# Agent attention with a grouped mixture of experts: another order for the first sorted tile, the placements, the maximum's chain and the factor loads

## The chip, the cores and the metric

The kernel runs on one core of one Trainium2 chip. Its five engines (PE for matmuls, DVE, ACT, POOL, and SP, which here only starts DMAs) run their own instruction streams side by side and wait for each other through semaphores. The metric is the device time of one execution in microseconds (us); lower is better. Every line number of the form L1582 is one of the kernel before, unless a listing of the changed kernel is meant.

## The reference

Four batches of 10048 tokens with 128 channels and 49 agents go through an attention in two steps. Its result, all 40192 rows, goes through a grouped mixture of experts with 4 groups of 4 experts, of which each row uses one:

```python
a2k = sm(agents, k)              # softmax over the 10048 keys, per agent
agent_v = a2k @ v                # 49 x 128
q2a = sm(q, agents)              # softmax over the 49 agents, per token
x = q2a @ agent_v
...
# g: argmax of x @ w_group; e: argmax of x @ w_expert[g]
out = g_w * e_w * (relu(x @ w1[g, e]) @ w2[g, e])
```

## The kernel before

The batches are taken in the order `SEQ = (1, 2, 3, 0)`. The first three are "own" batches. In such a batch all 20 tiles of 512 tokens go through the batch's most common expert, tile by tile, and the rows of other experts are dealt with at the very end. Since x is a mix of 49 agent values, the agent values are folded into w1: the kernel multiplies rows of exponentials (49 high and 49 low halves, so 98) by a folded w1, and what has been left out of the softmax and the gates is one factor per token, applied at the end. The last batch (`SORTED`) is routed instead: its rows are written in the order of their experts into `sorted_rows` in DRAM, and read back as 22 sorted tiles.

**A unit** is 128 of the 1024 hidden columns of one tile. Its first step is two matmuls into a PSUM bank `ph<-et,wbuf`; ACT makes the relu `hh`, DVE the low half `hl` (its "eviction", after which the bank is free; there are three such banks), and the second step is three matmuls `po<-hh` x2 and `po<-hl`. The second step of a unit comes eight units after its first (`LAG`). Tiles 11 to 19 of the third own batch, and the sorted tiles, run their units in groups of four. Three own batches make 480 units.

**Beside the units** everything else is made: scores and maxima of the next batch's keys (`key_scores`, `key_max`), the subtraction of the maximum from them (`value_less`, DVE `S<-S,mb`), exponentials, products with v, the query rows (`query_split`, L939) and their turning (`turned`, L1001), the choice of experts, and the placements. Each is a generator, a lane, and a planner at build time (`advance`, L1902) steps them after each unit. `clock[0]` counts units. A step that yields a number waits for that many units; `lag()` is 2. A lane may step when it is behind its share (`QUEUE`, `TOTALS`), within a budget of time per unit on DVE and ACT. The Tile framework then puts the instructions into each engine's stream.

**The maximum's chain** (`key_max`, L485) ends the score pass of a batch: DVE reduces to `mx`, PE transposes it (`at<-cp,mx`), DVE reduces again and makes `dg`, PE spreads it to all partitions, and only then can the subtractions and with them the value steps begin.

**Placements** (`placing`, L1378, DMA at L1384): each of the 79 blocks of 128 rows is written by one indirect DMA that POOL issues. They are the lane p3, which `advance` steps apart from the others, in four of five units and at the end in five of eight:

```python
if y["live"] and part > y["start"] and (clock[0] % 5 if part < NOWN - 1 + GROUPED / OT else clock[0] % 8 not in (0, 3, 6)):
    step(y)
```

**The end of the own batches** is prepared by `ahead` (L2037): when the last agent lane has ended, it queues the weights of the first sorted tiles (`weights`, `next_weights`, L1571: `wbuf<-wdr`, in halves, one half every `APART` = 4 units). When no lane is live, it issues four fetches of sorted tiles at once (`begin`, `fetch`, L1582: `er<-sorted_rows`, 512 tokens each). From the sixth unit after that, it turns one tile at a time (`next_turn`, `turn`: four transposes on PE `at<-ident,er`, a copy on ACT, strips by DMA at L1596), until two are turned. A fetch reads any row of its tile, so it comes after all placements. The first sorted unit comes some 30 units later.

**Output of an own tile:** `factors` (L1684) loads the per-token factors, spread to all partitions, into a buffer `oo` (L1698, `oo<-cwt`); after the last unit of the tile `out_rows` (L1701) multiplies `po` into it on DVE (`oo<-po,oo`) and stores it (L1706, `cols<-oo`). There are three buffers `oo`, so a load waits for the store of the tile three before. Nearly all these DMAs go out from SP, in the order of its stream; an instruction that waits there holds all behind it.

## Time and profile before

| | us |
|---|---|
| median of 3 runs | 869.18 (869.06 to 869.6) |
| profiled execution | 871.62 |
| its span (first to last instruction) | 869.8 |
| PE busy | 816.4 (94%) |
| DVE busy | 697.7 (80%) |
| ACT busy | 587.2 (68%) |
| POOL busy | 467.6 (54%) |
| mean granted clock of PE | 0.982 of full speed |

An engine's busy time is what its instructions take; the rest of the span it stood idle, for the reasons that the view of waits names. [...] DMA transfers run beside the engines, on 16 DMA engines; they moved 183 GB/s on the mean.

### The profile page before, as it was taken

Reading aid. Unit: us, or ns where it says so; the run is one execution under the profiler, and the core shown is the slowest. Engines: PE = TensorE matmul, PEld = TensorE weight load, DVE = VectorE, ACT = ScalarE, POOL = GpSimd, SP = SyncE. Lnnn points to the kernel's source line nnn. Section 1 sums busy time; section 2 is a strip of 40 time slices with the busy share of each in tenths; the row PEclk is TensorE's granted clock in tenths of the full one; section 3 lists DMA queues with packets and bytes.
Section 4 is the critical chain, followed back from the end, with each engine's and each line's share of the span. In section 5 each row is a group of like instructions: output and inputs, shape, how many; then the busy total and the mean of one; then the engine's idle time right before and its main releaser. Section 6 shows DMA issues by size and latency. Waiting matters only on the chain.

```text
span 869.8 us, 21556 instructions
## 1 busy us (share of the span) xinstructions
PE 816.4 (94%) x7993; PEld 475.3 (55%) x7994; DVE 697.7 (80%) x1455; ACT 587.2 (68%) x1094; POOL 467.6 (54%) x630
## 2 busy tenths in 40 slices
PE   4889799999999899989999999999997999999996
PEld 3746444455545455545545555544443477777775
DVE  7767589978799887898888799999794776666674
ACT  6567767876778778787777877765554555555552
POOL 4268747546638548675654437867450024444454
PEclk9979989999999999999999999999998999999999
DMA  9668738839496666866557324555865245555542
GB/s 356 273 213 226 221 116 213 246 110 201 149 279 175 178 205 197 226 171 170 155 170 206 111 83 128 162 169 167 258 224 183 78 144 192 181 167 195 173 140 97
DMA packets 92091, 158.92 MB, mean 183 GB/s; under 512 B 38688, under 2 KB 51012, under 8 KB 91976
## 3 DMA queue, kind: packets, MB, share of 16 engines
q1 hardware_dynamic: 86824, 147.15, 56.2%
q0 software_dynamic: 5152, 10.30, 3.6%
q8 instruction: 64, 1.05, 0.5%
q14 instruction: 51, 0.42, 0.2%
HBM read 107.81 MB, written 40.35 MB: 170 GB/s over the span
## 4 chain that ended last, share of the span: by engine, by line
PE 44%; issue 17%; DVE 14%; POOL 10%; ACT 6%; DMA 6%; SPq 1%; POOLq 1%; ACTq 0%; DVEq 0%
PE po L150 22%; PE ph L150 13%; PE at L150 9%; POOL out L1717 9%; DVE hl L150 5%; ACT hh L150 2%; DMA vf<-v 2%; DVE vl L150 2%; POOL xl L375 1%; DMA xf<-kT 1%; DMA oo<-cwt 1%; DMA cwt<-cwc 1%; ACT xh L150 1%; DVE mq L150 1%; DMA er<-sorted_rows 1%
## 5 line engine op out<-in xcount | busy, mean ns | idle before, releaser
L150 DVE SCALAR_TENSOR_TENSOR hl<-ph,hh 128x512 f16<-128x512 f32 (+1 forms) x500 | 332.0, 678 | 108.4 <-ACT hh L150 106.1
L150 PEld LDWEIGHTS <-wbuf 128*128 128x128 f16 (+2 forms) x2740 | 239.1, 98 | 300.6 <-issue 57.6
L150 ACT ACTIVATE hh<-ph 128x512 f16<-128x512 f32 (+1 forms) x500 | 287.2, 591 | 168.3 <-PE at L150 104.0
L150 PE MATMUL po<-hh,wbuf 128*128 128x512 f16 (+1 forms) x960 | 286.8, 379 | 0.0
L150 PE MATMUL ph<-et,wbuf 98*128 98x512 f16 (+3 forms) x870 | 263.5, 379 | 18.3 <-DVE hl L150 17.3
L375 POOL TENSOR_TENSOR xl<-xf,xh 128x256 f16<-128x256 f32 x278 | 182.0, 689 | 105.0 <-ACT xh L150 104.7
L150 PE MATMUL po<-hl,wbuf 128*128 128x512 f16 (+1 forms) x480 | 181.6, 378 | 0.0
L1717 POOL DMA_INDIRECT out<-oo,er x82 | 80.1, 976 | 134.5 <-DVE oo L150 76.6
L150 PE MATMUL po<-wbuf,hh 128*128 128x128 f16 x1312 | 116.6, 219 | 0.0
L150 PE MATMUL po<-wbuf,hl 128*128 128x128 f16 x656 | 112.9, 219 | 0.0
L150 PEld LDWEIGHTS <-hh 128*128 128x128 f16 x1312 | 99.2, 98 | 9.0 <-issue 9.0
L1384 POOL DMA_INDIRECT sorted_rows<-rows,slot x79 | 78.8, 997 | 40.6 <-issue 19.0
L150 ACT ACTIVATE xh<-xf 128x640 f16<-128x640 f32 (+1 forms) x110 | 82.3, 756 | 20.9 <-PE at L150 13.7
L150 DVE SCALAR_TENSOR_TENSOR hl<-at,hh 128x512 f16<-128x512 f32 (+1 forms) x100 | 67.9, 679 | 0.0
L150 PEld LDWEIGHTS <-hl 128*128 128x128 f16 x656 | 64.2, 98 | 0.0
L150 ACT ACTIVATE hh<-at 128x512 f16<-128x512 f32 (+1 forms) x100 | 60.4, 604 | 0.0
L968 POOL TENSOR_TENSOR rows<-ef,rows 128x245 f16<-128x245 f32 (+1 forms) x62 | 42.6, 710 | 28.6 <-ACT rows L150 28.6
L605 POOL TENSOR_TENSOR shl<-S,shl 128x245 f16<-128x245 f32 (+2 forms) x51 | 37.3, 753 | 31.1 <-ACT shl L150 31.1
L150 DVE TENSOR_TENSOR oo<-po,oo 128x512 f32<-128x512 f32 (+1 forms) x60 | 40.4, 674 | 15.1 <-PE po L150 8.4
L150 PEld LDWEIGHTS <-xh 128*128 128x128 f16 x1166 | 43.0, 98 | 12.6 <-issue 3.4
L150 DVE SCALAR_TENSOR_TENSOR vl<-vf,vh 128x640 f16<-128x640 f32 (+2 forms) x51 | 44.4, 878 | 6.2 <-ACT vh L150 5.5
L150 PE MATMUL at<-agh,xh 128*128 128x49 f16 x553 | 43.5, 185 | 1.5 <-issue 1.5
(345 smaller groups left out, 1033.7 us busy)
## 6 DMA issues: line engine op xcount, KB each, us to landing
vf<-v SPq DMA_DIRECT2D x28, 645.0 KB
xf<-qT SPq DMA_DIRECT2D x27, 640.0 KB
xf<-kT SPq DMA_DIRECT2D x25, 640.0 KB
cols<-oo SPq DMA_DIRECT2D x57, 256.0 KB
oo<-cwt SPq DMA_DIRECT2D x55, 256.0 KB
wbuf<-wdr SPq DMA_DIRECT2D x22, 512.0 KB
erow<-rows SPq DMA_DIRECT2D x12, 640.0 KB
wbuf<-wdr SPq DMA_DIRECT2D x22, 320.0 KB
```

Source lines behind the costliest of these rows:

```text
L150: ins = f(*a, **k)
L375: pool.tensor_sub(out=xl[:, a:z], in0=xf[:, a:z], in1=xh[:, a:z])
L605: pool.tensor_sub(out=sl[0:m, y][:, z], in0=x[:, z], in1=sh[0:m, y][:, z])
L968: pool.tensor_sub(out=x0[:, a:z, NA:2 * NA], in0=ef[:, a:z], in1=x0[:, a:z, 0:NA])
L1384: ins = pool.indirect_dma_start(out=sorted_rows[:, :], out_offset=bass.IndirectOffsetOnAxis(ap=at, axis=0), in_=x, in_offset=None, bounds_ ...
L1717: ins = pool.indirect_dma_start(out=out, out_offset=bass.IndirectOffsetOnAxis(ap=to, axis=0), in_=y, in_offset=None, bounds_check=N - 1, o ...
```

## The change

No instruction is added or taken away on any engine. What changes is the order and what is waited for:

- The first sorted tile is fetched alone as soon as all lanes have ended, and three more follow at 4, 8 and 12 units behind it. The turns come 12 and 14 units after the first fetch.
- The placement lane gains 2/3 of a placement per unit from its start, whether or not a placement is there to be made; what has come due is made one per unit.
- In `key_max` the two waits of `lag()` become `lag() + 2` and `lag() + 1`, and `lag()` units are added behind it; `value_less` waits a unit.
- `query_split` waits, before it takes a rows buffer, until that buffer's last turn and store are 6 units back.
- The factor load of a tile gets a dependency on the last multiply before it in the program, which puts it behind that tile's store.

```diff
+LANDED = 12
...
         vec.tensor_reduce(out=mx, in_=st["most"].rearrange("p c a -> p a c"), axis=AX.X, op=ALU.max)
...
-        yield lag()
+        yield lag() + 2
...
         vec.tensor_scalar(out=dg, in0=identf[0:NA, 0:NA], scalar1=ma, scalar2=None, op0=ALU.mult)
-        yield lag()
+        yield lag() + 1
...
             vec.tensor_sub(out=x, in0=x, in1=mb[0:m].broadcast_to([m, y.stop - y.start, NA]))
-        yield
+        yield 1
...
         yield from key_max(b, 0, n, False)
+        yield lag()
...
+                while len(made) >= RWB and not forced[0] and any(len(y) <= len(made) - RWB or clock[0] < y[len(made) - RWB] for y in (emptied, stored)):
+                    yield 0
+                made.append(r)
                 st["rows", r] = rp.tile([P, ST, 2 * rw], F16, name="rows", bufs=RWB)
...
+    multiplied = []
...
-        sync.dma_start(out=o[:, 0:n].rearrange("p a c -> p (a c)"),
-                       in_=cwt[SEQ.index(x["b"])][t:t + n].rearrange("(o t) p -> o (t p)", o=1).broadcast_to([P, n * P]))
+        ins = sync.dma_start(out=o[:, 0:n].rearrange("p a c -> p (a c)"),
+                             in_=cwt[SEQ.index(x["b"])][t:t + n].rearrange("(o t) p -> o (t p)", o=1).broadcast_to([P, n * P]))
+        for y in multiplied:
+            tc.add_manual_dep(ins.ins, y.ins.name, mybir.DependencyInfo(mybir.DependencyClass.Sync, mybir.DependencyReason.DATA),
+                              reason="the store of the tile before goes first")
...
-            vec.tensor_mul(out=o[:, 0:n], in0=po[:, 0:n], in1=o[:, 0:n])
+            multiplied[:] = [vec.tensor_mul(out=o[:, 0:n], in0=po[:, 0:n], in1=o[:, 0:n])]
...
                 over.add(i)
-                if y["live"] and part > y["start"] and (clock[0] % 5 if part < NOWN - 1 + GROUPED / OT else clock[0] % 8 not in (0, 3, 6)):
+                if part > y["start"]:
+                    y["due"] = y.get("due", 0) + bool(clock[0] % 3)
+                if y["live"] and y["done"] < y.get("due", 0):
                     step(y)
...
         if not fetched and not any(y["live"] for y in lanes):
-            while fetched < AHEAD:
-                begin()
+            begin()
             begun.append(clock[0])
-        elif fetched and len(turned_up) < AHEAD_TURNS and clock[0] > begun[-1] + LANDING - 2:
+        elif fetched and fetched < AHEAD and clock[0] >= begun[-1] + APART * fetched:
+            begin()
+        elif fetched and len(turned_up) < min(fetched, AHEAD_TURNS) and clock[0] >= begun[-1] + LANDED + 2 * len(turned_up):
             next_turn()
```

**First place: SP around the first sorted fetch**, near the end of the own batches (`wbuf_90` and `wbuf_91` are two weight buffers; a TENSOR_LOAD and an ISA row read a register with the address that the next DMA uses). Before, three more fetches of the same kind follow the last row:

```order
L1571 DMA wbuf_91<-wdr 128x640
L1569 TENSOR_LOAD sli
L1571 ISA
L1571 DMA wbuf_91<-wdr 128x1024
L1698 DMA oo<-cwt_142 128x512
L1706 DMA cols<-oo 128x512
L1580 TENSOR_LOAD sli
L1582 ISA
L1582 DMA er<-sorted_rows 128x512
```

After, from behind the stores of the last expert product on:

```order
L1586 TENSOR_LOAD sli
L1588 ISA
L1588 DMA wbuf_90<-wdr 128x640
L1597 TENSOR_LOAD sli
L1599 ISA
L1599 DMA er<-sorted_rows 128x512
L1586 TENSOR_LOAD sli
L1588 ISA
L1588 DMA wbuf_90<-wdr 128x1024
L1005 DMA rest<-et 19x512 x3
```

The first fetch moved from behind four weight loads to behind the first half of one; the next three stand singly between the weights and strips. On PE the four transposes of the first turn stand behind the 446th `po<-hl` of the own units' second steps instead of the 447th; the last expert products on DVE stand four evictions later than before.

**Second place: SP around the factor loads**, in the first own batch. The numbers tell the buffers apart: three of them are used in turn, so `oo_6827` is in the buffer of `oo_6304`, and after the change `oo_6921` in that of `oo_6440`. Before:

```order
L1706 DMA cols<-oo_6304 128x512
L1010 DMA_TRANSPOSE et_6840<-rows_5668 128x3x128
L974 DMA erow3_138<-rows_6487 128x1280
L1698 DMA oo_6827<-cwt1_141 128x512
L266 DMA vf_6785<-v 128x1290
L258 DMA xf_6805<-qT 128x1280
L1010 DMA_TRANSPOSE et_7642<-rows_6487 128x4x128
L1706 DMA cols<-oo_6467 128x512
L1698 DMA oo_7040<-cwt1_141 128x512
```

After:

```order
L1728 DMA cols<-oo_6440 128x512
L1717 DMA oo_6766<-cwt1_141 128x512
L267 DMA vf_6866<-v 128x1161
L1027 DMA_TRANSPOSE et_7799<-rows_6437 128x4x128
L1728 DMA cols<-oo_6626 128x512
L1717 DMA oo_6921<-cwt1_141 128x512
L259 DMA xf_7089<-qT 128x1280
```

Before, a load stands shortly behind the store of the very buffer that it writes. Now it stands right behind the store of the tile after that one: `oo_6766` stands behind the store of `oo_6440`, and the buffer that it writes was stored one tile earlier.

**Third place: DVE around the subtractions** `S<-S,mb` (the maximum taken from the scores, 10 blocks of 49 columns each, the last ones smaller) between the evictions `hl`. Before, evictions 238 to 243, in the second own batch:

```order
L150 SCALAR_TENSOR_TENSOR hl<-ph,hh 128x512
L150 TENSOR_TENSOR S<-S,mb 128x490
L150 SCALAR_TENSOR_TENSOR hl<-ph,hh 128x512
L150 TENSOR_TENSOR S<-S,mb 128x490 x2
L150 TENSOR_TENSOR S<-S,mb 128x392
L150 SCALAR_TENSOR_TENSOR vl<-vf,vh 128x640
L150 SCALAR_TENSOR_TENSOR hl<-ph,hh 128x512
L150 SCALAR_TENSOR_TENSOR vl<-vf,vh 128x640
L150 SCALAR_TENSOR_TENSOR hl<-ph,hh 128x512
L150 TENSOR_TENSOR oo<-po,oo 128x512
```

After, at the same evictions:

```order
L151 SCALAR_TENSOR_TENSOR hl<-ph,hh 128x512
L151 TENSOR_TENSOR S<-S,mb 128x490
L151 SCALAR_TENSOR_TENSOR hl<-ph,hh 128x512
L151 TENSOR_TENSOR S<-S,mb 128x490
L151 SCALAR_TENSOR_TENSOR hl<-ph,hh 128x512
L151 TENSOR_TENSOR oo<-po,oo 128x512
L151 SCALAR_TENSOR_TENSOR hl<-ph,hh 128x512
L151 TENSOR_TENSOR S<-S,mb 128x490
L151 SCALAR_TENSOR_TENSOR hl<-ph,hh 128x512
L151 TENSOR_TENSOR S<-S,mb 128x392
L151 TENSOR_TENSOR S<-S,mb 64x49
```

After, at evictions 53 to 58, in the first own batch, where the kernel before has these subtractions at evictions 55, 59, 64 and 65, one at a time:

```order
L151 SCALAR_TENSOR_TENSOR hl<-ph,hh 128x512 x4
L151 TENSOR_TENSOR S<-S,mb 128x490
L151 SCALAR_TENSOR_TENSOR hl<-ph,hh 128x512
L151 TENSOR_TENSOR S<-S,mb 128x490 x2
L151 TENSOR_TENSOR S<-S,mb 128x392
L151 SCALAR_TENSOR_TENSOR vl<-vf,vh 128x640
L151 SCALAR_TENSOR_TENSOR hl<-ph,hh 128x512
L151 SCALAR_TENSOR_TENSOR vl<-vf,vh 128x640
```

The three subtractions and the value split behind one eviction are spread at the first place, and stand together at the other. Around eviction 64 two multiplies `oo<-po,oo` stand behind one eviction after the change; before, they stood behind evictions 61 and 64.

## Rows read from the trace of the kernel before

**Rows 1.** The page: busy us of each engine and its share of the span; the granted clock of TensorE.

```profile
PE 816.4 (94%) x7993; PEld 475.3 (55%) x7994; DVE 697.7 (80%) x1455; ACT 587.2 (68%) x1094; POOL 467.6 (54%) x630
...
PEclk9979989999999999999999999999998999999999
```

**Rows 2.** Waits of PE: who waits, for what, us in total, times, longest.

```profile
PE ph L150 <- DVE hl L150: 17.3, 21, 2.7
...
PE at L150 <- DMA er<-sorted_rows: 4.4, 1, 4.4
PE at L150 <- DVE mx L150: 3.3, 2, 2.4
```

**Rows 3.** Timeline of PE, 656 to 675: start, us, instruction [idle before it <- releaser].

```profile
657.62 0.38 PE L150 MATMUL po<-hl,wbuf 128*128 128x512 f16 x1
...
658.27 0.38 PE L150 MATMUL po<-hl,wbuf 128*128 128x512 f16 x1
663.04 0.60 PE L150 MATMUL at<-ident,er 128*128 128x128 f16 x4 [4.40 <-DMA er<-sorted_rows]
...
665.15 1.49 PE L150 MATMUL ph<-et,wbuf 128*128 128x512 f16 x3
...
670.62 0.81 PE L150 MATMUL ph<-et,wbuf 128*128 128x512 f16 x3
...
674.50 0.81 PE L150 MATMUL ph<-et,wbuf 128*128 128x512 f16 x3
```

**Rows 4.** Windows: busy us of PE, PEld, DVE, ACT, POOL; granted clock, DMA share, GB/s.

```profile
660.00:662.00 2.00, 0.00 (x0) 0.00 (x0) 0.00 (x0) 0.00 (x0) 0.00 (x0) 0.93 0.96 354
662.00:664.00 2.00, 0.96 (x6) 0.69 (x7) 0.00 (x0) 0.32 (x1) 0.00 (x0) 0.50 0.75 287
```

**Rows 5.** Timeline of SP's DMA queue, 644 to 671.

```profile
645.41 0.35 SPq L1538 DMA_DIRECT2D wdr<-wbuf  x1
...
648.70 1.22 SPq L1571 DMA_DIRECT2D wbuf<-wdr  x2
...
656.89 3.11 SPq L1582 DMA_DIRECT2D er<-sorted_rows  x4
```

**Rows 6.** The same view of SP, 101 to 104.

```profile
102.32 1.29 SPq L1698 DMA_DIRECT2D oo<-cwt  x3
```

**Rows 7.** Timeline of DVE, 104 to 109.

```profile
106.48 0.69 DVE L150 TENSOR_TENSOR oo<-po,oo 128x512 f32<-128x512 f32 x1 [4.93 <-DMA oo<-cwt]
```

**Rows 8.** Timeline of PE, 388 to 392.

```profile
391.23 0.59 PE L150 MATMUL ph<-et,wbuf 98*128 98x512 f16 x2 [2.30 <-DVE hl L150]
```

**Rows 9.** Windows, columns as in group 4, 392 to 396.

```profile
392.00:394.00 2.00, 2.00 (x7) 0.73 (x5) 2.00 (x4) 1.33 (x3) 2.00 (x4) 0.52 0.51 103
394.00:396.00 2.00, 2.00 (x35) 1.36 (x33) 1.00 (x3) 0.23 (x1) 2.00 (x4) 0.63 0.89 350
```

**Rows 10.** Timeline of PE, 107 to 116.

```profile
107.82 0.59 PE L150 MATMUL ph<-et,wbuf 98*128 98x512 f16 x2 [2.68 <-DVE hl L150]
...
110.11 0.42 PE L150 MATMUL at<-cp,mx 128*49 128x128 f32 x1 [0.88 <-DVE mx L150]
```

**Rows 11.** Timeline of DVE, 381 to 392.

```profile
386.35 2.98 DVE L150 TENSOR_TENSOR S<-S,mb 128x490 f32<-128x490 f32 x3
389.26 1.32 DVE L150 SCALAR_TENSOR_TENSOR vl<-vf,vh 128x640 f16<-128x640 f32 x1
```

**Rows 12.** Waits of SP's DMA queue: us in total, times, longest.

```profile
SPq L1698 <- DMA cols<-oo: 91.8, 34, 5.9
```

**Rows 13.** Waits of POOL: us in total, times, longest.

```profile
POOL rows L953 <- DMA et<-rows: 19.6, 5, 7.2
```

**Rows 14.** Instructions on sorted_rows: count, ns min/median/max, first and last start.

```profile
L1384 POOL DMA_INDIRECT sorted_rows<-rows,slot x79: 971/977/1302, 523.8 to 651.6; - x79
```

**Rows 15.** Timeline of POOL, 584 to 590.

```profile
586.24 0.98 POOL L1384 DMA_INDIRECT sorted_rows<-rows,slot  x1 [0.30 <-DVE pf L150]
```

**Rows 16.** Windows of the instructions on hh alone: PE, PEld, DVE, ACT; clock, DMA.

```profile
536.40:632.30 95.90, 47.50 (x160) 0.00 (x0) 50.02 (x77) 43.21 (x76) 1.00 0.63 191
```

More of the change, by code (lines that the diff above doesn't have):

```diff
@@ L974, in query_split @@
             sync.dma_start(out=erow[b].rearrange("(p t) c -> p t c", t=NTP)[:, r * ST:(r + 1) * ST], in_=st["rows", r].bitcast(I32))
+            stored.append(clock[0] + TURNED)
     def grouped(b, i):
@@ L999, in rest_of, with turned_own @@
             sync.dma_start(out=rest[j * STRIP:j * STRIP + REST, 0:w], in_=et[DUP:NA, 0:w])
+    made, emptied, stored = [], [], []
     def turned(b, i):
+        if b != SORTED:
+            yield from turned_own(b, i)
+            if (i + 1) * TQ % ST == 0:
+                emptied.append(clock[0] + TURNED)
+            return
+        yield from turned_own(b, i)
+    def turned_own(b, i):
         n = min(TQ, NT - i * TQ)
@@ L2062, in build @@
                 ahead()
+                while fetched < AHEAD:
+                    begin()
                 while len(turned_up) < AHEAD_TURNS:
```

## The prediction

> **What bounds the kernel now.** I read the page's busy line first: PE is busy for 94% of the span, so only what stops or slows PE can move the time by much [rows 1]. The clock line under it has weak digits in slices 3, 6, 19, 31 and 40. Next come the waits of PE. What the reader should see there is that no engine holds PE up steadily: its longest single wait after the first stage, 4.40 us, is for the fetch of sorted rows; waits for DVE's evictions make 17.3 us in 21 pieces, and the maximum of k makes two [rows 2]. The timeline of PE at the 4.40 us shows what else it costs: the turn begins at 663.04 instead of 658.65, where the last second matmul before it ends, and until the group at 670.62 everything is drawn out [rows 3]. [...] So I cost each edit by the PE gap it closes or opens and by the slow stretch behind the gap.
>
> **The first sorted fetch.** In the SP timeline, SP stores the last expert product at 645.41, loads wbuf at 648.70, and comes to the four fetches only at 656.89 [rows 5]; PE has the first at 663.04, so 6.15 us from issue to use. In the new order (first pair of listings) fetch 0 stands behind only half of the first wbuf load. The last expert store is made up to four evictions later than before, at 3.88/4 = 0.97 us each (670.62 to 674.50 is a group of four at full clock [rows 3]). So the store is at 645.4 to 649.3; the wbuf load follows it by 3.29 us (648.70 less 645.41), half of its 1.22 us is 0.6, and with the register loads fetch 0 is issued at about 649.8 to 653.3. From issue to use I take between 4.2 us (three factor loads issued at 102.32, multiply at 106.48 [rows 6, 7]) and 6.15 us: fetch 0 is there at 654.0 to 659.5. PE wants it at 658.0, since the turn stands one unit's second matmuls (0.65 us, 657.62 to 658.27 [rows 3]) earlier in PE's order than before. The middle, 656.7, is in time: **-4.40 us**, with 1.5 us of it lost at the late end. Fetch 1 is some 3 us behind (half a load, three strip copies at 0.6, the fetch), at 657.2 to 662.5, and is wanted at 658.9. Residual 0 to 3.6; I take **+0.5**, since the middle is only 1 us late and the second matmuls between the turns cover part of that.
>
> With the gap goes the slow stretch. The group 665.15 to 670.62 took 5.47 us against 3.88, so 1.6; the piece 663.04 to 665.15 took 2.11 where full clock makes it about 1.05. Together **-2.65 us**. If a gap of 2 us or more stays, the stretch stays with it: after the 2.30 us gap at 391.23 the clock was 0.52 and 0.63 in the next windows [rows 8, 9].
>
> [...]
>
> **The maximum's chain.** At 110.11 PE stands 0.88 us for the maximum of the first key batch [rows 10]. Two more units move that transpose behind two further units' matmuls, 0.97 us each even at full clock [rows 3], so 1.9 us, more than the wait: **-0.88**. The other batches show no such wait but one early one that the change does not touch. In all, the chain is three units longer, and so the value steps behind it start that much later; no wait of PE stands at their start, 0.
>
> **Subtractions on DVE.** Over the last batch's keys three subtractions and a value split came in one block behind an eviction: 2.98 us from 386.35 and 1.32 from 389.26 [rows 11]. PE ran out of evicted banks for 2.30 us [rows 8] and then lost (1-0.52)x2 + (1-0.63)x2 = 1.7 us to the clock [rows 9]. The third pair of listings shows that block dissolved at evictions 238 to 242 and the same block, three subtractions and a split, new at eviction 57 (about 139 us by the trace of before). So -4.0 there and between 0 and +4.0 at the new place; around eviction 64 the multiplies of two tiles are now neighbours where they were three evictions apart, which costs between 0 and +1.4 (two multiplies at 0.69 [rows 7]). A block like the old one costs the same if POOL is as busy beside it; I take **0** for all of it, bounds -4.0 and +1.4.
>
> **The factor loads.** SP stood 91.8 us in 34 waits at the factor load behind the store of the tile before it [rows 12]. The new dependency makes each load follow a store one tile later, when the buffer has been free for long (second pair of listings), and SP's queue behind it (value loads, turns) moves. But the only load from SP that stands among the longer waits of PE is the sorted fetch [rows 2], so I take **0**; a later load could be late for its multiply by up to a tile, and such a wait costs PE up to the 2.68 us that it did at 107.82 [rows 10]. On the other side, SP's freed queue can shorten only the other small waits of PE, a us together. The bounds are -1 and +2.7. The new wait before the query split keeps POOL from standing for a rows buffer (19.6 us in 5 waits, 7.2 the longest [rows 13]): the planner takes steps of other lanes in its place. PE never waited for those rows by itself, and a step that is late is still forced before its tile, so 0.
>
> **Placements.** The 79 placements take 0.977 us each [rows 14], one per 1.28 us with the 0.30 between [rows 15]. They start later in the program: eight to nine units at 95.9/76 = 1.26 us [rows 16], so at 523.8+10.7 = 534.5 instead of 523.8. They are denser: only six row splits of about 0.7 us stand between them. 79 x 1.28 + 4.3 = 105.4 us, so the last is issued by about 640, where it was 651.6 [rows 14]. Fetch 0 at 650 has 10 us of cover. Beyond feeding the fetch they are worth **0**.
>
> **The sum.** -4.40 + 0.5 - 2.65 - 0.88 = -7.43 us. The profiled execution took 871.62 us (span 869.8), which makes 864.2 of it. That execution lies 2.4 above the median 869.18, and the prediction is for the median: 869.18 - 7.43 = **861.8 us**. With the bounds of the unpriced terms and the late end of fetch 1 (+3.1), its own range is up to 865; down to 858 where the subtractions give most of their 4.0.
>
> **Rivals.**
> 1. *The fetch stays late.* The weights are still ahead of it, and fetch 1 has a whole load between. For it: DMA moves 354 GB/s in 660 to 662, while PE waits [rows 4], so transfers then queue for bandwidth. Against it: fetch 0 goes 4 to 7 us earlier. If 2 to 4 us of waiting stay, the clock falls too, and the gain is 0.9 plus at most 2.4: 869.18 - 3.3 to 869.18 - 0.9, so 866 to 868.5 us.
> 2. *New DVE blocks.* The one at eviction 57 costs the 4.0 us of the old one, and the clock falls behind it, while the one removed at 238 shows up elsewhere: 861.8 + 4 to + 8, so 866 to 870 us. For it: the listing shows the block. Against: POOL's work beside it differs, and a 3 us block costs PE only what its three banks don't cover.
> 3. *Slower: placements are drawn out.* SP now stands at fetch 0 behind the last placement, and placements without gaps meet DVE, busy 80% of the span [rows 1]. With a period p the last ends at 534.5 + 79p + 4.3. The gain starts to go at p = 1.38 (the last ends at 648, and its rows must land before the fetch at 650), is gone at 1.45 (653 us, where the last one ended before), and the kernel is slower from about 1.47. At the longest placement in the row, 1.302 + 0.30 = 1.60, it ends at 665, the rows are there at 672, nine later than 663.04, and the time is 869.18 + 9 - 0.9 = 877 us. Against it: the same row has a median of 0.977 with a minimum of 0.971 in that very stretch, so busy DVE did not stretch them. [...]
> 4. *More gain.* The block at 238 goes and the new one costs nothing: 861.8 - 4.0 - 0.5 (no residue at fetch 1) - 1 (the other small waits), so 855 to 858 us.
>
> That the change does not do what it says is excluded for the order: the listings show each edit. Whether it fires in time is rival 1.
>
> **How the numbers follow.** Forecast 0.55 (858 to 865). Rival 1 0.17, rival 2 0.12, rival 3 0.08, rival 4 0.08. A measurement of this kernel can tell about 0.2%, 1.7 us, from no change: faster is under 867.4, slower over 870.9. Faster: 0.55 + 0.11 (of rival 1) + 0.04 (of 2) + 0.08 = 0.78. Same: 0.05 + 0.05 + 0.01 = 0.11. Slower: 0.01 + 0.03 + 0.07 = 0.11. The range of 8 in 10 takes in the forecast, rival 1, the lower half of rival 2 and the upper half of rival 4: 857.0 to 868.8.
>
> **What would show it.** Right: the PE wait for er gone or under 1 us, no clock below 0.9 between 655 and 672, the first sorted group in 3.9 us; SP issuing fetch 0 at 650 to 653; the last placement before 645; no 0.88 us wait at the first maximum; SP's wait at the factor load far under 91.8. Wrong: an er wait above 2 us with a slow stretch behind it (rival 1); a gap for hl with half clock near 139 us (rival 2); placements with a median above 1.1 us (rival 3).

## The result and the profile after

| | before, us | changed, us | ratio (95% interval) |
|---|---|---|---|
| first set of runs | 869.28 (869.06 to 869.6) | 859.78 (859.23 to 860.47) | 0.9891 (0.9874 to 0.9908) |
| beside experiments e6 to e8 | 869.58 (866.39 to 871.65) | 862.10 (859.48 to 865.0) | 0.9895 (0.9858 to 0.9931) |

The change makes the kernel faster by 9.5 us in the first set, 7.5 in the second. The forecast was 7.4 (861.8 us), with 857.0 to 868.8 as its range. One remark is needed to read the experiments: each of their four sets ran on another chip, and in two of them (e1 to e4, and e9 to e11) the kernel before itself took 889 us where it takes 869 in the others, so each time below is compared with the kernel before of its own set, by the ratio.

The page of the changed kernel, busy time and granted clock; the rows that answer are [rows 1]:

```profile
PE 809.2 (94%) x7993; PEld 472.6 (55%) x7994; DVE 699.4 (82%) x1455; ACT 587.9 (69%) x1094; POOL 464.7 (54%) x630
...
PEclk9979999999999999999999999999999999999998
```

The weak digits at slices 6 and 31 are gone, and there is a new one at slice 40, where the kernel ends. (Of the slices that the prediction called weak in the page before, 3, 6 and 31 have a digit below 9; 19 and 40 have a 9.) The waits of PE (us in total, times, longest; compare [rows 2]):

```profile
PE ph L151 <- DVE hl L151: 15.2, 18, 2.8
...
PE at L151 <- DVE mx L151: 2.6, 1, 2.6
...
PE at L151 <- DMA er<-sorted_rows: 0.2, 1, 0.2
```

The wait for er has shrunk from 4.4 to 0.2 us; the waits for evictions are about what they were. The timeline of PE at the first two turns, against [rows 3]:

```profile
651.82 0.38 PE L151 MATMUL po<-hl,wbuf 128*128 128x512 f16 x1
652.04 0.39 PE L151 MATMUL at<-ident,er 128*128 128x128 f16 x4
...
653.25 0.40 PE L151 MATMUL at<-ident,er 128*128 128x128 f16 x4 [0.18 <-DMA er<-sorted_rows]
...
654.14 0.81 PE L151 MATMUL ph<-et,wbuf 128*128 128x512 f16 x3
...
658.02 0.81 PE L151 MATMUL ph<-et,wbuf 128*128 128x512 f16 x3
```

The first turn at 652.04 waits for nothing, the second for 0.18 us, and the group that follows takes 658.02 - 654.14 = 3.88 us, which is full clock. The window there confirms it, where [rows 4] had 0.50 (busy us of PE, PEld, DVE, ACT, POOL; granted clock as a share of full speed, DMA share, GB/s):

```profile
650.00:654.00 4.00, 3.82 (x27) 1.63 (x25) 2.54 (x5) 2.87 (x6) 0.00 (x0) 1.00 0.66 179
```

The timeline of SP ahead of it, against [rows 5]:

```profile
641.08 0.36 SPq L1555 DMA_DIRECT2D wdr<-wbuf  x1
...
644.64 0.35 SPq L1588 DMA_DIRECT2D wbuf<-wdr  x1
645.50 0.34 SPq L1599 DMA_DIRECT2D er<-sorted_rows  x1
646.36 0.33 SPq L1588 DMA_DIRECT2D wbuf<-wdr  x1
...
649.98 0.35 SPq L1599 DMA_DIRECT2D er<-sorted_rows  x1
```

SP stores the last expert product at 641.08, issues half of the first weights at 644.64 and fetch 0 at 645.50. That is 6.5 us before PE wants it, where before the first fetch went out 1.8 us before (656.89, and PE was ready at 658.65).

The whole program can be weighed in one sum. PE's idle time, plus the half of its busy time that it spends at half clock (where three matmuls took 1.49 us that take 0.81 at full clock [rows 3]), up to its last matmul: 57.1 and 55.0 us in two traces of the kernel before (the second is e6), 47.6 and 50.8 in two of the changed one. PE's last matmul ends at 862.1 and 859.9 us in the former, at 849.5 and 855.3 in the latter, so that without them 804.5 to 805.0 us are left in three of the four traces, and 801.9 in the first of the changed kernel. So where PE stood and where its clock was down account for the gain between the traces, but for some 3 us in that one. (The second pair of traces lies closer together than its medians: they are of executions that took 869.89 and 865.00 us, 4.9 apart where the medians are 7.5.)

### The profile page after: what moved, and what is told of

It reads as the page before. It is cut to its first block, busy times and chain, and to the rows that moved or that the text cites. A ratio compares the mean times of both kernels' runs of the same rounds, so it can differ in the third digit from the quotient of the medians.

```text
span 857.5 us, 21557 instructions
## 1 busy us (share of the span) xinstructions
PE 809.2 (94%) x7993; PEld 472.6 (55%) x7994; DVE 699.4 (82%) x1455; ACT 587.9 (69%) x1094; POOL 464.7 (54%) x630
## 5 line engine op out<-in xcount | busy, mean ns | idle before, releaser
L376 POOL TENSOR_TENSOR xl<-xf,xh 128x256 f16<-128x256 f32 (+1 forms) x278 | 181.6, 688 | 88.5 <-ACT xh L151 87.0
L606 POOL TENSOR_TENSOR shl<-S,shl 128x245 f16<-128x245 f32 (+2 forms) x51 | 34.8, 704 | 52.5 <-ACT shl L151 52.5
L973 POOL TENSOR_TENSOR rows<-ef,rows 128x245 f16<-128x245 f32 (+1 forms) x62 | 40.5, 676 | 31.0 <-ACT rows L151 30.7
L151 PE MATMUL at<-agl,xh 128*128 128x49 f16 x553 | 43.3, 184 | 0.0
```

Source lines behind the costliest of these rows:

```text
L151: ins = f(*a, **k)
L376: pool.tensor_sub(out=xl[:, a:z], in0=xf[:, a:z], in1=xh[:, a:z])
L606: pool.tensor_sub(out=sl[0:m, y][:, z], in0=x[:, z], in1=sh[0:m, y][:, z])
L973: pool.tensor_sub(out=x0[:, a:z, NA:2 * NA], in0=ef[:, a:z], in1=x0[:, a:z, 0:NA])
```

## The experiments

### What the fetch part needs: e1, e2, e3 and e9

Theory A says that the time between fetch and turn decides; theory C, my prediction's, that the fetch standing alone ahead of the weights does; theory B that the earlier end of the placements does.

**e1, e9**: the changed kernel with the fetch part undone: four fetches at once, turns from the sixth unit after them.

```diff
-            begin()
+            while fetched < AHEAD:
+                begin()
             begun.append(clock[0])
-        elif fetched and fetched < AHEAD and clock[0] >= begun[-1] + APART * fetched:
-            begin()
-        elif fetched and len(turned_up) < min(fetched, AHEAD_TURNS) and clock[0] >= begun[-1] + LANDED + 2 * len(turned_up):
+        elif fetched and len(turned_up) < AHEAD_TURNS and clock[0] > begun[-1] + LANDING - 2:
...
```

> The changed kernel with the fetch part undone: four fetches at once when the lanes have ended, turns from the sixth unit after. All else as changed; on PE the first turn stands behind the 439th second step instead of the 446th, so PE is there at about 645.1, while SP issues the first fetch at 645.5 as before this edit. Theory A (what counts is the time between fetch and turn): PE waits 4 to 6 us for er, and a half-clock stretch of about 7 us follows it, 2.7 us lost; 859.8 + 7 to 9 = 867 to 869 us. Theory B (the wait went because the placements ended earlier and the fetch is issued earlier in the program): no wait above 1 us, 859 to 861 us.

Measured: 896.08 us, ratio 1.0081 (1.0048 to 1.0113). SP's and PE's timelines at the turn:

```profile
671.37 2.84 SPq L1599 DMA_DIRECT2D er<-sorted_rows  x4
...
674.73 0.40 PE L151 MATMUL at<-ident,er 128*128 128x128 f16 x4 [2.59 <-DMA er<-sorted_rows]
```

PE is ready at 672.1 (674.73 less its wait of 2.59), the fetch goes out at 671.37 and is used at 674.73: 3.36 us after its issue, and 2.59 of them PE waits. The repetition gave ratio 1.0111 (1.0082 to 1.0141) at 899.64 us:

> The kernel of the first experiment again, in a set of runs where the kernel before takes about 869 us, so that the fetch part can be priced. Theory A: PE is at the turn at about 645, SP issues the first of the four fetches at 645.5 and it takes 3.4 us or more to land (671.37 to 674.73 in the first experiment), so a wait of 4 to 6 us, 1.7 to 2.7 us lost to the clock behind it: ratio 0.9975 to 1.001 against the kernel before, where the changed kernel has 0.9895. Theory B: no such wait, ratio 0.99.

```profile
672.96 2.83 SPq L1599 DMA_DIRECT2D er<-sorted_rows  x4
...
676.19 0.50 PE L151 MATMUL at<-ident,er 128*128 128x128 f16 x4 [2.00 <-DMA er<-sorted_rows]
```

Again 3.2 us from issue to use (672.96 to 676.19), and 2.00 us of waiting. This set was of the 889 us kind too, so the price of the fetch part in whole time, for which e9 was made, was not measured where the kernel before takes 869 us. Theory B, by which no wait should be left, falls with both: the placements ended early here too. The waits were under the 4 to 6 us of theory A, because the fetch lands sooner than I took it to and because PE came to the turn 0.8 and 1.2 us after the issue, where theory A had it there 0.4 us before. Nor did the slow stretch that theory A expected follow each time: behind the 2.59 us PE kept its full clock in e1, behind the 2.00 in e9 it had 3.4 us of half clock.

**e2**: `LANDED = 6` in place of 12, with the fetch still alone.

> The changed kernel with turns 6 and 8 units after the first fetch instead of 12 and 14; the first tile is still fetched alone. Theory A: waits for er of 4 to 6 us at the first turn, and up to 3 us at the second, whose fetch is issued four units later, with the half-clock stretch behind: 867 to 871 us. Theory C (my prediction's: a fetch that stands alone ahead of most of the weights is there in about 5 us, and that is what removes the wait): the wait shrinks to under 2 us, 860 to 863 us.

Measured: 895.38 us, ratio 1.0075 (1.0028 to 1.0122):

```profile
671.33 0.34 SPq L1599 DMA_DIRECT2D er<-sorted_rows  x1
...
675.93 0.35 SPq L1599 DMA_DIRECT2D er<-sorted_rows  x1
...
674.19 0.40 PE L151 MATMUL at<-ident,er 128*128 128x128 f16 x4 [1.69 <-DMA er<-sorted_rows]
...
679.66 0.40 PE L151 MATMUL at<-ident,er 128*128 128x128 f16 x4 [2.05 <-DMA er<-sorted_rows]
```

Both turns wait, 1.69 and 2.05 us, the second for a fetch that went out at 675.93, four units later; the clock stays full behind both. From issue to use the lone fetch took 2.86 us (671.33 to 674.19), so standing alone is worth some 0.4 to 0.5 us against e1 and e9. The first wait is under the 2 us that theory C allowed, so this run alone does not decide; e3 does.

**e3**: four fetches at once, turns as late as in the changed kernel.

```diff
-            begin()
+            while fetched < AHEAD:
+                begin()
             begun.append(clock[0])
```

> The changed kernel with the four first tiles fetched at once, as before the change, and turns still 12 and 14 units after. Theory A: no wait for er above 0.5 us, 859 to 861 us, as the changed kernel. Theory C: the first fetch is no longer alone, three more and the weights share the DMA engines with it; a wait of 2 us or more and a slow stretch, 863 us or more.

Measured: 892.08 us, ratio 1.0038 (1.0013 to 1.0062); by the medians 4.0 us faster than e1 and 3.3 faster than e2 of the same set (their single times overlap):

```profile
671.55 2.84 SPq L1599 DMA_DIRECT2D er<-sorted_rows  x4
...
678.04 0.39 PE L151 MATMUL at<-ident,er 128*128 128x128 f16 x4
```

With the same fetch time as e1, and all four fetches in a row, the turn at 678.04 waits for nothing, and its second neither. So theory A holds and C falls: with the late turn there is no wait although four fetches go out at once, with the early one there is a wait even for a lone fetch. The fetch that stood alone (e2) waited, the one that did not (e3) didn't. All three kernels keep the early end of the placements.

### The placements: e4 and e12

```diff
-                if part > y["start"]:
-                    y["due"] = y.get("due", 0) + bool(clock[0] % 3)
-                if y["live"] and y["done"] < y.get("due", 0):
+                if y["live"] and part > y["start"] and (clock[0] % 5 if part < NOWN - 1 + GROUPED / OT else clock[0] % 8 not in (0, 3, 6)):
                     step(y)
```

> The changed kernel with the placement part undone (four of five units, then five of eight). The last placement comes at unit 468 instead of 438 and the first fetch at 469 instead of 449; the turns follow at 482 and 483, 10 units before the first sorted unit. Theory A: the fetch still has 13 units to its turn; no wait, 859 to 861.5 us. Theory B: the fetch now stands behind the placements again, later than in the kernel before, and PE waits 2 us or more with a slow stretch: 863 us or more.

> The kernel of the fourth experiment again (placements paced as in the kernel before, all else as changed). There it was the fastest of its set, 18 us faster than the kernel that differs from it in the placements and in the four fetches at once. If the placements' density is what costs where the kernel before takes 889 us, and is worth nothing where it takes 869 us, this version keeps a ratio of 0.982 to 0.992 in either: at 869 us that of the changed kernel (0.9895), at 889 us that of the fourth experiment (0.9845). If the denser placements are part of the changed kernel's gain (Theory B), the ratio at 869 us is 0.993 or more, with a wait for er.

Measured where the kernel before takes 869.65 us: 862.04, ratio 0.9906 (0.9881 to 0.9931), no different from the changed kernel's 0.9891 and 0.9895. Four fetches stand in a row there too, 5 us behind the start of the last placement (661.3), and PE has them in time:

```profile
666.53 3.35 SPq L1599 DMA_DIRECT2D er<-sorted_rows  x4
...
674.49 0.39 PE L151 MATMUL at<-ident,er 128*128 128x128 f16 x4
```

So the denser placements are no part of the gain that these runs can tell. In the changed kernel the turn stands where it stood (behind the 446th `po<-hl` and not the 447th), and its distance from the fetch comes from the earlier fetch, as predicted; in e12 it comes from a later turn (behind the 466th), and that does as well. Where the kernel before takes 889.29 us, the same kernel took 873.92, ratio 0.9845 (0.9796 to 0.9895), and was 18 us faster than e3. The two differ in the placements and in whether one or four fetches go first, and the latter can't cost that much as e3's turns wait for nothing. The windows from 540 to 660 us show where the difference lies; first the changed kernel and e12 of the 869 us sets, then e3 and e4 of the 889 us set:

```profile
540.00:660.00 120.00, 118.09 (x730) 54.08 (x729) 106.28 (x288) 73.59 (x141) 72.78 (x76) 1.00 0.65 200
```

```profile
540.00:660.00 120.00, 117.86 (x728) 54.17 (x727) 108.36 (x294) 73.28 (x139) 74.33 (x77) 1.00 0.64 193
```

```profile
540.00:660.00 120.00, 100.93 (x599) 45.60 (x600) 91.35 (x256) 59.11 (x113) 72.89 (x77) 0.96 0.51 155
```

```profile
540.00:660.00 120.00, 113.31 (x686) 51.96 (x683) 104.64 (x284) 68.59 (x131) 70.16 (x73) 0.99 0.57 179
```

PE is busy for 118 of 120 us in the first two with either pacing. In the other set it loses 17 us with the dense placements (100.93) and 5 with the old ones. The placements themselves (count, ns min/median/max, first and last start), of the changed kernel and of e3:

```profile
L1401 POOL DMA_INDIRECT sorted_rows<-rows,slot x79: 964/973/1399, 527.6 to 632.9; - x79
```

```profile
L1401 POOL DMA_INDIRECT sorted_rows<-rows,slot x79: 966/972/1147, 528.5 to 652.4; - x79
```

Their medians are the same, 0.973 and 0.972 us, and the longest of e3 is the shorter one (1.147 for 1.399). But their period went from (632.9 - 527.6)/78 = 1.35 to (652.4 - 528.5)/78 = 1.59 us, and PE, DVE, ACT and POOL stood now and then. Two waits of PE in e3 show the pattern, one of them for nothing that the trace shows ("issue"):

```profile
586.21 0.38 PE L151 MATMUL po<-hl,wbuf 128*128 128x512 f16 x1 [0.60 <-issue]
588.26 0.59 PE L151 MATMUL ph<-et,wbuf 98*128 98x512 f16 x2 [1.67 <-DVE hl L151]
```

In e1, e2, e3 and e9, the kernels whose order up to there is that of the changed kernel, the 320th `po<-hl` starts at 500 to 501 us, as it does in the changed kernel (500.2); the loss begins where the placements do. The density alone isn't it: the kernel before has the old pacing and took 20 us more in these sets (889 for 869), e4 took 12 more (873.92 for e12's 862.04), e3 some 30. What slowed the engines in that stage in these sets, on two chips other than those of the 869 us sets, and why more placements per time go with a greater loss, stays open: it was not tried, and there is no trace of the kernel before from such a set. The changed kernel itself did not run in such a set; e3, which differs from it in the fetches alone, took 1.0038 of the kernel before there. The version of e4 and e12 is the one that kept its gain in both.

### The maximum's chain and the subtraction's unit: e7, e10, e11

**e7** undoes the three chain edits (`lag() + 2`, `lag() + 1`, `yield lag()` behind `key_max`) and leaves the unit in `value_less`.

> The changed kernel with the three edits of the maximum's chain undone (the one unit in the subtraction step stays). Theory A: PE waits 0.9 us for the first maximum again, and the half-clock stretch near 108 us is 6.8 us instead of 3.4, so 0.9 + 1.7 = 2.6 us slower than the changed kernel up to the first own tile's end; DVE steps fall otherwise, which moves it by 2 us either way. Theory D (the chain is worth nothing; the shorter stretch came from a luckier fall of the clock): same time up to 126 us as the changed kernel within 0.5 us.

Measured: 883.16 us, ratio 1.0152 (1.0113 to 1.0192), 21 us slower than the changed kernel of the same set, e5. Neither theory saw that. The waits of PE:

```profile
PE ph L151 <- DVE hl L151: 25.0, 28, 3.5
...
PE at L151 <- DVE mx L151: 3.0, 2, 2.4
PE at L151 <- ACT xh L151: 2.5, 1, 2.5
PE at L151 <- POOL xl L376: 2.5, 3, 1.6
```

The wait for the maximum is back by only 0.6 us in total (3.0 for 2.4 in e5, two waits for one). What is new is elsewhere: late splits of loads (xh, xl: 5.0 us), evictions at 25.0 us where e5 has 19.1. Two places in the timelines, first a value split on DVE and PE's wait behind it, then a key load's split on ACT:

```profile
146.28 0.82 DVE L151 SCALAR_TENSOR_TENSOR vl<-vf,vh 128x640 f16<-128x640 f32 x1 [3.63 <-ACT vh L151]
```

```profile
147.76 1.01 PE L151 MATMUL ph<-et,wbuf 98*128 98x512 f16 x2 [3.48 <-DVE hl L151]
```

```profile
250.38 2.46 ACT L151 ACTIVATE xh<-xf 128x640 f16<-128x640 f32 x4 [4.62 <-DMA xf<-kT]
```

DVE stands 3.63 us for the high half of a value load at 146.28, with the evictions queued behind it, and PE 3.48; ACT stands 4.62 for a key load. PE's idle time up to its last matmul is 54.6 us where e5 has 45.1, and the half clock behind the gaps costs 12.3 where e5 has 5.7: 16 of the 17 us that lie between their two spans. In the stretch that the theories were about, e7 is 1.3 us behind e5 at the 40th `po<-hl` (125.1 and 123.8 us), and its half clock near 108 us lasts 6.8 us, as theory A had it.

**e10** undoes `yield 1` in `value_less` alone, **e11** both.

> The changed kernel without the unit's wait in the subtraction step (value_less), the longer maximum's chain kept. The planner puts the last expert products at evictions 421, 433 and 437 as in the kernel before, and the first placement at unit 351. Theory E (the subtraction step's unit and the longer chain belong together; the run with the first and without the second was 21 us slower than the changed kernel): this half alone is also off, 866 us or more, ratio 0.996 or more. Theory F (the longer chain alone is what counts, the unit is what did harm in that run): same as the changed kernel or better, ratio 0.985 to 0.991.

> The changed kernel with all edits of the maximum's chain and of the subtraction step undone: on DVE the side work then stands behind the same evictions as in the kernel before, and fetch, placements, rows buffers and factor loads are as changed. My prediction's sum: the 7 us at the fetch stay gained, the 0.88 us wait at 109 and the block of subtractions near 388 us with its slow stretch come back; 861 to 864 us, ratio 0.991 to 0.994. Theory F: without the longer chain it is as slow as the run without it, ratio 1.01 or more.

Measured: e10 908.16 us, ratio 1.0199 (1.0168 to 1.0229), e11 902.56, 1.0161 (1.0134 to 1.0188). Both ran where the kernel before takes 888.8 us, and both place still earlier (from 522.7 and 522.0 us on) and densely, so their totals don't price the chain, and the expected ratios can't be held against them. Their first 320 units can be read: the 320th `po<-hl` starts at 506.6 in e10 and 504.6 in e11, against 506.5 and 503.7 in two traces of the kernel before, 500.2 and 503.8 of the changed one, and 520.3 in e7. Only e7 falls out. So one half of the pair without the other is harmful in one direction, the unit without the chain; the other half alone, both and neither lie between 500.2 and 506.6, and two traces of one kernel lie up to 3.6 us apart there, so that these single traces show no difference between them. The mechanism in e7 (other loads fall late when the steps that free their buffers move) is what its rows suggest; that it must come with this pair was not shown.

### The whole and the factor loads: e5, e6 and e8

> The changed kernel itself, beside the kernel before, to have both in one set of runs: in the runs of the first four experiments the kernel before took 889 us and not 869, and PE, DVE, ACT and POOL all stood at times for nothing that the trace shows between 530 and 660 us. If that is a matter of the runs and the same for every kernel, this one keeps its gain of 9 to 10 us over the kernel before (ratio 0.989). If the denser placements bring it (Theory P), it loses its gain where the kernel before takes 889 us: ratio 1.00 to 1.01, with stalls of all engines between 530 and 640.

> The kernel before itself, for its trace in the same set of runs. Ratio 1.00. If the runs are as the first four were, the stalls of all engines lie between 540 and 655 us, where its placements are, and the 4.40 us for er and the half-clock stretch behind it are there too. If they are as those of the prediction, it takes 869 us and its span differs from the 869.8 of the profiled execution by the 2 us that that one lay above its median.

Measured in one set: the changed kernel 862.10, ratio 0.9895 (0.9858 to 0.9931); the kernel before 869.59, 1.0007 (0.9984 to 1.003), with a span of 868.0. The kernel before again waits 4.73 us for er, 6.43 us after the issue at 655.35, with 3.4 us of half clock behind it and not 6.8; the changed one waits 1.28 at the second turn and keeps its full clock (the turn of e6 first, then the second turn of e5):

```profile
661.78 0.40 PE L150 MATMUL at<-ident,er 128*128 128x128 f16 x4 [4.73 <-DMA er<-sorted_rows]
```

```profile
659.05 0.40 PE L151 MATMUL at<-ident,er 128*128 128x128 f16 x4 [1.28 <-DMA er<-sorted_rows]
```

This set being of the 869 us kind, the question about the 889 us kind was not answered by it.

**e8** takes the dependency away (the loop over `multiplied` runs over nothing); only SP's order changes.

> The changed kernel without the dependency of the factor load; only the order on SP changes. My forecast took the dependency for nothing: same time as the changed kernel within 1 us, although SP's wait at the factor load goes back to 60 to 100 us. Rival: the freed SP queue brought a part of what the prediction did not foresee (the time came out 2 us lower): 1.5 to 4 us slower than the changed kernel, with more PE waits behind late turns or value loads.

Measured: 862.23 us, ratio 0.9897 (0.9867 to 0.9927): the same as the changed kernel, as far as four runs of each can tell (859.82 to 863.94 and 859.48 to 865.0). SP's wait at the factor load, of the changed kernel and of e8, against [rows 12]:

```profile
SPq L1717 <- DMA cols<-oo: 6.0, 2, 4.1
```

```profile
SPq L1717 <- DMA cols<-oo: 68.2, 29, 5.8
```

So 62 us of waiting on SP come back without showing in the time.

## Why the prediction was right, and where it was off

**The fetch (-4.40 + 0.5) and the slow stretch (-2.65)** came as said: the wait went from 4.40 to 0.18 us and the stretch behind it is gone, with the prediction's 2.65 us for the stretch 6.9 us together. In the second pair of traces it is less: 4.73 - 1.28 = 3.45 us of waiting and half of 3.4 us of half clock, 5.2 together.

Three steps below it were off. I took 4.2 to 6.15 us from issue to use; it is 3.2 to 3.4 for four fetches behind half a weight load (e1, e9), 2.9 for one (e2), and 3.6 at the second fetch (e5: issued at 655.43, used at 659.05). I took the second fetch to go out 3 us behind the first; it was 4.5 (645.50 and 649.98). And I put the gain down to the fetch's place ahead of the weights, which the earlier end of the placements was to make possible. The place goes with a shorter fetch, 3.2 to 3.4 us with the same early turns for 6.15 and 6.43 in the kernel before, but then 2.0 to 2.6 us of waiting are left (e1, e9, on other chips); e3 and e12 show that the distance of the turn from the fetch, 13 units for 6, leaves no wait, with the fetch alone or not and the placements dense or not. And "if a gap of 2 us or more stays, the stretch stays with it" did not hold: e1 and e2 keep full clock behind 2.59 and 2.05 us.

Whether the weights ahead of the fetch make it longer was not tried by itself. The kernel before, with four weight loads ahead, took the longer times (6.15 and 6.43 us); with the half load that is left ahead of the fetch in e1 it was 3.4 us, less than I had taken. The residue at the second turn, taken at 0.5, was 0.2, 1.3 and, in e8, 1.8; the last two are over the 1 us that the prediction named as its sign of being right.

**The maximum's chain (-0.88)**: the wait at 110.11 is gone, the transpose comes two units later at 112.14 with none; the rows against [rows 10]:

```profile
107.22 0.59 PE L151 MATMUL ph<-et,wbuf 98*128 98x512 f16 x2 [2.81 <-DVE hl L151]
...
112.14 0.27 PE L151 MATMUL at<-cp,mx 128*49 128x128 f32 x1
```

The half clock behind the 2.8 us gap lasted 3.4 us instead of 6.8, which looked like another 1.7 us. One pair of traces can't show that: the second trace of the kernel before has 3.4 there, and those of e8 and e12 none at all, after nearly the same gap. Taken together the traces still point that way. With the old chain the half clock lasts 6.8, 3.4, 6.8 and 6.8 us (the kernel before twice, e7, e11), with the longer one it lasts 3.4 us four times (the changed kernel twice, e3, e10) and stays out five times (e1, e4, e8, e9, e12), each time behind a gap of 2.4 to 3.0 us. The means, 6.0 and 1.5 us, differ by 2.2 us of lost time, which the prediction had at nothing; that the chain does it was not shown, as it was not tried by itself with the side work left in its place. What the prediction mis-sized is what the chain is worth beside the rest of the change: "in all, the chain is three units longer [...] 0" left out that with the subtraction's unit in and the chain out the kernel is 21 us slower (e7). In the direction that was asked, before to after, the wait itself came out about right.

**Subtractions (0)**: the loss and the gain both came. On DVE the new block at eviction 57, and the one at eviction 150, which the prediction had only as a possible place of rival 2:

```profile
135.69 2.73 DVE L151 TENSOR_TENSOR S<-S,mb 128x490 f32<-128x490 f32 x3
138.35 0.81 DVE L151 SCALAR_TENSOR_TENSOR vl<-vf,vh 128x640 f16<-128x640 f32 x1
...
264.70 1.17 DVE L151 TENSOR_TENSOR S<-S,mb 128x490 f32<-128x490 f32 x1
...
266.02 0.86 DVE L151 TENSOR_TENSOR S<-S,mb 128x490 f32<-128x490 f32 x1
266.81 1.26 DVE L151 SCALAR_TENSOR_TENSOR vl<-vf,vh 128x640 f16<-128x640 f32 x1
```

PE behind each of them:

```profile
139.81 0.59 PE L151 MATMUL ph<-et,wbuf 98*128 98x512 f16 x2 [0.15 <-DVE hl L151]
...
268.73 0.80 PE L151 MATMUL ph<-et,wbuf 98*128 98x384 f16 x2 [2.69 <-DVE hl L151]
```

The first block takes 2.73 + 0.81 us on DVE and costs PE 0.15 us, far below the old one's 2.30. PE gets through three more units in both cases. But the old block was 0.76 us longer (2.98 + 1.32), DVE began it 0.64 us later against PE (0.83 us after a `ph` of PE, here 0.19), and here PE had 0.9 us of other matmuls, key scores from 138.75 on, before it came to the next unit: 2.3 us together. POOL's work beside a block, which rival 2 named, went with longer subtractions, but not each time: in the kernel before two of them took 1.24 us with POOL idle (from 119.57 on), the three of the old block 2.98 us with POOL busy (from 386.35 on), and one took 0.66 us at 382.23, beside POOL's `xl`. The second costs 2.69 us, with a slow stretch behind it:

```profile
268.00:270.00 2.00, 1.27 (x4) 0.55 (x4) 2.00 (x5) 0.55 (x3) 2.00 (x4) 0.63 0.10 14
270.00:272.00 2.00, 2.00 (x6) 0.73 (x5) 2.00 (x4) 1.13 (x3) 2.00 (x3) 0.52 0.34 131
```

So the 4.0 us at 388 went, and about as much came at 266: (1 - 0.63) x 1.27 + (1 - 0.52) x 2 = 1.4 us on top of 2.69. Neither figure is net, and the second is of one trace. Between 370 and 400 us PE's waits for evictions fell from 2.8 to 0.8 us; between 255 and 280 they rose from 1.9, in three small waits, to 2.7. In e6 and e5 they went from 2.8 to 1.5 and from 1.8 to 3.5, and behind the same gap, 2.70 us at 270.36, e5 keeps its full clock:

```profile
270.00:272.00 2.00, 1.64 (x9) 0.87 (x9) 2.00 (x4) 1.11 (x3) 2.00 (x5) 1.00 0.00 0
```

With the 1.7 us of clock that went at 388 (e6 has that stretch too), the term comes to about -1.5 us in the first pair and -1.3 in the second. That the 0 came near was luck: two numbers that I had only bounded nearly cancelled. The block at 266 is rival 2 by half, and it helps to keep the time above rival 4's.

**Factor loads (0)**: e8 shows no difference. **Placements (0)**: nor does e12, in the sets where the kernel before takes 869 us. The last one started at 632.9 and not 651.6, near the 640 of the prediction less the 6 us by which all stood earlier.

**Rival 3** (placements drawn out, slower) did not happen in the set of the prediction. In the 889 us sets something near it did: not the single placement, but its period grew to 1.59 us, past the 1.47 that I had named, and the versions with dense placements came out between 1.0038 and 1.0199 of the kernel before. A busy DVE that stretches the single placement isn't the cause that these rows show, as placements kept 0.972 us and PE and ACT stood too.

**The rows buffers' wait (0)** was not tried by itself; POOL's waits for them are not shorter for it (15.4 and 6.2 us behind turns, where 19.6 was before [rows 13]).

The 2 us by which the first set's time lies under the forecast stay unexplained (the 3 us that the sum of idle time and slow clock leaves over in that set's trace may be part of it, and so may the subtractions and the shorter half clock behind the chain); the second set gives 7.5 us of gain where 7.4 were forecast. There the fetch part gave about 5 us by the traces where 6.55 were forecast, so terms taken at 0, or the scatter of the runs, made up the rest: the total is closer than its parts.

## What to carry to other kernels

A wait of the main engine for a transfer has two cures, an earlier issue and a later use; ask for the later use first where the result is not needed for another 30 units: in e12 it did as well as the earlier issue and cost nothing that shows. Price the slow clock behind a gap with the gap, but from more than one trace, since its length varies between executions of one kernel (6.8 and 3.4 us behind the gap near 105 us in two of the kernel before). And undo the parts of a change singly before keeping them: here the fetch part makes 5 to 7 of the 7.5 to 9.5 us by the traces, the factor loads were worth nothing that shows, the subtraction's unit without the longer chain cost 21 us, and the denser placements made no difference in one set of runs, while in another the version with them was 18 us slower (e3 against e4, which differ in the fetches too).

## What the runs showed of the hardware that I had not expected

- After nearly the same gap, 2.4 to 3.0 us long and begun at 103 to 106 us, PE ran at half clock (granted 0.50) for 6.8 us or 3.4 us (the kernel before in two executions), 3.4 us (the changed one in two) and not at all (e8, e12, and e1, e4 and e9).
- In two sets, on two chips, PE, DVE, ACT and POOL stood at times in the stage of the indirect DMAs, for nothing that the trace shows (in e3 from 560 to 675 us ACT 8.5 us in 6 waits before `hh`, DVE 5.7 in 4 before `hl`, POOL up to 2.7 before one placement, where the changed kernel has 0.3); PE's busy time from 540 to 660 us was 100.93 us in e3 and 101.84 in e9, for 118.09 in the changed kernel of the first set. With placements at the old pace it was 113.31 (e4).
- The first of four fetches behind half a weight load is used 3.2 to 3.4 us after its issue (e1, e9), a lone one 2.9 (e2); behind four weight loads it took 6.15 us [rows 3, 5] and 6.43 (e6).
